# Linear attention feeding an MLP: the head of the program reordered, its transposes of batch 1 moved from DMA to TensorE, and later loads issued behind stages

## The chip, the cores and the metric

The kernel runs on one core of one Trainium2 chip. The time is device microseconds (us) of that core, as the median of the runs. Runs of one kernel mostly lie within 0.4% of their median. In these kernels the results of TensorE lie in PSUM, in tiles of one or two banks, until another engine takes them out (an eviction).

TensorE does matrix products and transposes, ScalarE (ACT in the profile) the exponentials, VectorE (DVE) maxima, divisions and copies, GpSimd (POOL) one multiply of the MLP and the scaling of v. GpSimd also issues the loads, and SyncE (SP) issues DMA transposes and output writes.

## The reference

```python
def phi(x):                                    # Hedgehog feature map
    proj = einsum('bhsd,df->bhsf', x, w_phi)   # 8 batches, 8 heads, seq 576, d 64, f 128
    proj = proj - max(abs(proj), axis=-1, keepdims=True)
    return concatenate([exp(proj), exp(-proj)], axis=-1)
q_p, k_p = phi(q), phi(k)
kv  = einsum('bhsf,bhsd->bhfd', k_p, v)
z   = sum(k_p, axis=2)
num = einsum('bhsf,bhfd->bhsd', q_p, kv)
den = einsum('bhsf,bhf->bhs', q_p, z)[..., None] + 1e-06
x   = (num / den).transpose(0, 2, 1, 3).reshape(4608, 512)
# then the MLP on all 4608 rows
h = x @ w_in                                   # 512 -> 2048
g = where(h > 0, h, exp(min(h, 0)) - 1)        # ELU
return g @ w_out                               # 2048 -> 512
```

## The kernel before

The heads are worked in 16 groups of four, two groups for each batch (n = 0 to 15, batch n // 2). The MLP is worked in nine chunks of 512 rows. For one group the stages are these: transpose k and q (so that d lies on the partitions); `stage_k` (project k, row maxima, exponentials, scale v); `stage_qmax` (project q only for its row maxima, split the maxima in two bf16 parts, transpose them to `mT`); `stage_q` (project q again, subtract the maxima by matmul, exponentials); `stage_kv`; `stage_pn` (numerator and denominator, divide, transpose x for the MLP).

```python
PE_TRANSPOSED = 2                    # groups 0 and 1 on TensorE, the others by DMA
pjp = psum_pool(bufs=2)              # two banks each: attention tiles
mpp = psum_pool(bufs=4)              # one bank each: MLP tiles

def pe_transpose(dst, blocks):       # on TensorE, in an attention tile
    tr = pjp.tile([P, 16, P], BF16, name="tr", tag="pj")
    for j, blk in enumerate(blocks):
        nc.tensor.transpose(tr[:, j, :], blk, ident)
    nc.vector.tensor_copy(dst, tr[:, 0:len(blocks), :])

# end of stage_qmax: the maxima of group n, transposed
if n < PE_TRANSPOSED:
    pe_transpose(mT, [mhl_2d])
else:
    nc.sync.dma_start_transpose(out=mT, in_=mhl_2d)

transposes(0)
for c in range(3): stage_k(0, c)
for c in range(3): stage_qmax(0, c)
transposes(1)
LAG = 3                              # an MLP chunk starts 3 pieces after its batch
for n in range(NG):
    pieces = []
    for c in range(3):
        pieces.append([(stage_q, n, c), (stage_qmax, n + 1, c)])
    pieces.append([(transposes, n + 2), (stage_kv, n)])
    pieces.append([(stage_k, n + 1, 0)])
    pieces.append([(stage_pn, n, 0)])
    pieces.append([(stage_k, n + 1, 1)])
    pieces.append([(stage_pn, n, 1)])
    pieces.append([(stage_k, n + 1, 2)])
    # loads of v of the next batch, k and q of the batch after it, are issued here
    # (on GpSimd; k, q and v have two buffers each)
    # after each piece, its share of 16 MLP pieces
    ...                              # cut: no n + 1 in the last group
```

An MLP piece is one first-layer tile (`moe_mm1`: four matmuls "ph", exponential on ScalarE, minimum on GpSimd, the rest of ELU on VectorE) or four second-layer matmuls (`moe_mm2`, "po"). A scheduler then orders each engine's instructions, and each engine takes them from its own queue.

## Time and profile before

| | us |
|---|---|
| median of 3 runs (lowest, highest) | 429.88 (429.65, 430.48) |
| span of the profiled execution | 429.5 |
| batch 0 complete: last copy of its transposed x ends | 68.9 |
| first q projection of group 2, 3, 4, 5 | 69.31, 89.76, 110.85, 132.94 |
| first q projection of group 15, the last | 346.57 |
| from there to the end (called the tail below) | 82.95 |

"First q projection" is the first matmul with the tile name pq of a group in the timeline. It is the milestone here. Here are the busy times from the page of the kernel before, and from its view of the DMAs (`--dma`) one group of issues; its last number is the median time from issue to landing.

```profile
PE 370.4 (86%) x3818; PEld 195.1 (45%) x3818; DVE 241.3 (56%) x405; ACT 246.5 (57%) x437; POOL 185.2 (43%) x249
...
mT<-mhl SPq DMA_TRANSPOSE x14, 3.7
```

The reader is to see that TensorE is the busiest engine with 370 of the 429.5 us of the span. The other 59 us are what a reordering can hope for, and they lie mostly in the first 75 us and in the waits between stages.

### The profile page before, as it was taken

To read this page: it belongs to the slowest core of one execution; us is meant where nothing else is said; L and a number is where in the kernel's file an instruction comes from. 1 tells how busy PE (TensorE), PEld (TensorE's weight loads), DVE (VectorE), ACT (ScalarE), POOL (GpSimd) and SP (SyncE) were. 2 spreads that over 40 slices of the span, in tenths; PEclk is the share of its full clock that TensorE was granted. 3 is DMA by queue.
4 is the path that set the end of the run, shared out by engine and by line. 5 is a ranking of instruction groups with operands and counts; after the bars stand their busy time and mean duration, and the time that the engine had idled before them with its cause. 6 is when DMAs were issued, how large, how long until landed. Compare 5 with 4: busy or idle time off the path is not lost.

```text
span 429.5 us, 9422 instructions
## 1 busy us (share of the span) xinstructions
PE 370.4 (86%) x3818; PEld 195.1 (45%) x3818; DVE 241.3 (56%) x405; ACT 246.5 (57%) x437; POOL 185.2 (43%) x249
## 2 busy tenths in 40 slices
PE   2467247889998999899989998999799989899995
PEld 2244233445453545354535453645354535344442
DVE  2646235876485648574857486648664853370630
ACT  1444416594777577747774777477657771451631
POOL 8612045382447245724572457145604570350620
PEclk9999657899999999999999999999999999999999
DMA  8999994359624982499259812853343003303113
GB/s 129 213 205 181 197 146 76 33 85 160 150 59 72 167 144 58 80 144 170 46 89 149 166 37 46 135 121 28 43 84 77 17 15 41 88 0 75 24 26 73
DMA packets 74619, 41.32 MB, mean 96 GB/s; under 512 B 54992, under 2 KB 69456, under 8 KB 74576
## 3 DMA queue, kind: packets, MB, share of 16 engines
q1 hardware_dynamic: 59232, 22.37, 29.1%
q0 software_dynamic: 15344, 18.35, 27.3%
q8 instruction: 30, 0.49, 0.5%
q14 instruction: 13, 0.11, 0.1%
HBM read 36.77 MB, written 9.44 MB: 108 GB/s over the span
## 4 chain that ended last, share of the span: by engine, by line
PE 51%; ACT 14%; POOL 11%; issue 11%; DVE 6%; DMA 6%; SPq 0%; POOLq 0%; ACTq 0%
PE po L185 21%; PE ph L163 14%; POOL e_sb L172 6%; ACT EK L270 5%; PE kv L372 5%; POOL vs L284 4%; DMA kT<-kn 4%; ACT e_sb L171 4%; ACT Eq L354 3%; PE pn L394 3%; PE pk L251 2%; PE pm L300 2%; DVE gT L175 2%; DVE mq L307 2%; DMA qn<-in_q_dram 1%
## 5 line engine op out<-in xcount | busy, mean ns | idle before, releaser
L163 PE MATMUL ph<-xT_sb,w_in_sb 128*128 128x512 bf16 x576 | 141.6, 385 | 14.3 <-DVE gT L175 12.9
L185 PE MATMUL po<-w_out_sb,gT 128*128 128x512 bf16 x576 | 137.8, 380 | 0.4 <-DVE gT L175 0.4
L175 DVE SCALAR_TENSOR_TENSOR gT<-e_sb,ph 128x512 bf16<-128x512 f32 x144 | 93.6, 683 | 65.6 <-POOL e_sb L172 65.6
L172 POOL TENSOR_SCALAR e_sb<-e_sb 128x512 f32<-128x512 f32 x144 | 86.5, 612 | 98.6 <-ACT e_sb L171 98.5
L171 ACT ACTIVATE e_sb<-ph 128x512 f32<-128x512 f32 x144 | 82.9, 608 | 45.8 <-PE ph L163 45.5
L284 POOL TENSOR_TENSOR vs<-vn,em 128x1152 bf16<-128x1152 bf16 x32 | 67.9, 2121 | 83.4 <-ACT em L281 83.3
L270 ACT ACTIVATE EK<-pk 128x768 bf16<-128x768 f32 x96 | 72.6, 813 | 35.7 <-DVE mk L242 35.6
L354 ACT ACTIVATE Eq<-pq 128x768 bf16<-128x768 f32 x96 | 74.0, 824 | 24.3 <-PE pq L344 24.2
L163 PEld LDWEIGHTS <-w_in_sb 128*128 128x128 bf16 x576 | 53.8, 99 | 72.6 <-issue 16.9
L185 PEld LDWEIGHTS <-gT 128*128 128x128 bf16 x576 | 52.2, 98 | 55.6 <-DVE gT L175 1.1
L307 DVE TENSOR_REDUCE mq<-pm 128x6 f32<-128x768 f32 x48 | 45.9, 957 | 49.5 <-PE pm L300 49.5
L194 ACT COPY o_sb<-po 128x512 f32<-128x512 f32 x36 | 21.1, 587 | 72.2 <-PE po L185 48.8
L242 DVE TENSOR_REDUCE mk<-pk 128x6 f32<-128x768 f32 x48 | 45.8, 953 | 12.4 <-PE pk L251 11.9
L394 PEld LDWEIGHTS <-Eq 128*128 128x128 bf16 x640 | 26.2, 102 | 8.4 <-issue 1.4
L251 PE MATMUL pk<-w_bd,kT 128*128 128x256 bf16 x144 | 26.3, 296 | 3.0 <-ACT EK L270 2.8
L372 PE MATMUL kv<-vs,EK 64*128 64x65 bf16 x1152 | 23.1, 198 | 5.3 <-POOL vs L290 4.2
L394 PE MATMUL pn<-kv_sb,Eq 128*128 128x65 bf16 x640 | 27.2, 200 | 0.3 <-DVE kv_sb L380 0.2
L300 PE MATMUL pm<-w_bd,qT 64*128 64x128 bf16 x288 | 18.0, 235 | 10.9 <-DMA qT<-qn 5.9
L406 DVE TENSOR_TENSOR xp<-pn,rec 128x640 bf16<-128x640 f32 x32 | 26.4, 824 | 1.1
L372 PEld LDWEIGHTS <-EK 64*128 64x128 bf16 x1152 | 20.9, 99 | 11.8 <-issue 4.3
L251 PEld LDWEIGHTS <-kT 128*128 128x128 bf16 x144 | 14.6, 105 | 15.5 <-issue 6.5
L334 PE MATMUL pq<-qT,w_bd 64*128 64x384 bf16 x96 | 17.2, 353 | 4.7 <-DVE mq L307 4.4
(42 smaller groups left out, 144.5 us busy)
## 6 DMA issues: line engine op xcount, KB each, us to landing
out_dram<-o_sb SPq DMA_DIRECT2D x72, 128.0 KB, 2.4
kn<-in_k_dram POOLq DMA_DIRECT2D x7, 576.0 KB, 6.1
qn<-in_q_dram POOLq DMA_DIRECT2D x7, 576.0 KB, 8.5
vn<-in_v_dram POOLq DMA_DIRECT2D x7, 576.0 KB, 6.7
w_in_sb<-in_moe_w_in_dram POOLq DMA_DIRECT2D x2, 1024.0 KB, 14.9
w_out_sb<-in_moe_w_out_dram POOLq DMA_DIRECT2D x2, 1024.0 KB, 31.4
xT_sb<-xp SPq DMA_TRANSPOSE x56, 2.4
kn<-in_k_dram POOLq DMA_DIRECT2D x2, 288.0 KB, 5.8
```

The source lines that it names most:

```text
L163: nc.tensor.matmul(ph, w_in_sb[:, ct, jt * P:(jt + 1) * P], xT_sb[:, ct, t0:t0 + CHUNK], start=(ct == 0), stop=(ct == N_CT - 1),)
L171: nc.scalar.activation(e_sb, ph, ACT.Exp)
L172: nc.gpsimd.tensor_scalar(e_sb, e_sb, 1.0, 0.0, op0=ALU.min, op1=ALU.max)
L175: nc.vector.scalar_tensor_tensor(gT[:, jt, :], e_sb, -1.0, ph, op0=ALU.add, op1=ALU.max)
L185: nc.tensor.matmul(po, gT[:, jt, tt * P:(tt + 1) * P], w_out_sb[:, jt, :], start=(jt == 0), stop=(jt == N_JT - 1),)
L251: nc.tensor.matmul(pj[:, 2 * i3:2 * i3 + 2, :].rearrange("p r f -> p (r f)"), kT[:, 3 * c + i3, :], w_bd.rearrange("p r f -> p (r f)"), st ...
L270: nc.scalar.activation(EK[:, sg, 6 * c:6 * c + 6, :], pj, ACT.Exp, scale=1.0 - 2.0 * sg)
L284: nc.gpsimd.tensor_tensor(vs[:, :, r, 0:D], natural["v", b][:, 2 * g + pr].unsqueeze(1).to_broadcast((P, 2, NS, D)), em[:, :, r].unsqueeze ...
L307: nc.vector.tensor_reduce(mq[:, 6 * c:6 * c + 6].rearrange("p (i r) -> p r i", r=2), pj[:, :, 0:3, :], axis=AX.X, op=ALU.max, apply_absolu ...
L354: nc.scalar.activation(Eq[:, sg, :, :, 3 * c * D:3 * (c + 1) * D].rearrange("p h r x -> p r h x"), pj[:, :, 0:3 * P].rearrange("p r (h x) ...
L372: nc.tensor.matmul(kv[:, hi, pr, sg, :], EK[rows, sg, pr * NS + s, :], vs[rows, sg, pr * NS + s, :], start=(s == 0), stop=(s == NS - 1),)
L394: nc.tensor.matmul(pn[:, hi, t, :], Eq[:, sg, hi, par, i0 * D:(i0 + 2) * D], kv_sb[:, hi, pr, sg, :], start=(sg == 0), stop=(sg == 1),)
```

## The change

The intent is to fill the loose first 75 us. The head becomes serial: batch 0 is run to its end first, so that the MLP can start early. Batch 1 (groups 2 and 3) is transposed on TensorE too, now in the MLP's PSUM banks, in parts of five. The k and q maxima of group 2 become a stage of their own with 4 MLP pieces. The loads of later batches are issued behind the stages that free their buffers. In the loop the piece with the transposes and kv is cut in two. In the last group, which has nothing to transpose, this leaves an empty piece, which only moves MLP pieces: those between kv and pn.

```diff
-    PE_TRANSPOSED = 2
+    PE_TRANSPOSED = 4
+    PE_TRANSPOSED_X = 2          # x of groups 0 and 1 on TensorE, as before
 ...
     def pe_transpose(dst, blocks):
-        tr = pjp.tile([P, 16, P], BF16, name="tr", tag="pj")
-        for j, blk in enumerate(blocks):
-            nc.tensor.transpose(tr[:, j, :], blk, ident)
-        nc.vector.tensor_copy(dst, tr[:, 0:len(blocks), :])
+        for j0 in range(0, len(blocks), 5):
+            part = blocks[j0:j0 + 5]
+            tr = mpp.tile([P, 8, P], BF16, name="tr", tag="mp")
+            for j, blk in enumerate(part):
+                nc.tensor.transpose(tr[:, j, :], blk, ident)
+            nc.vector.tensor_copy(dst[:, j0:j0 + len(part), :], tr[:, 0:len(part), :])
 ...
+    run(
+        [[(transpose_in, 0, "k")]] + thirds(stage_k, 0)
+        + [[(transpose_in, 0, "q")]] + thirds(stage_qmax, 0)
+        + [[(transpose_in, 1, "k")]] + thirds(stage_k, 1)
+        + thirds(stage_q, 0) + [[(transpose_in, 1, "q")]] + thirds(stage_qmax, 1)
+        + [[(stage_kv, 0)], [(stage_pn, 0, 0)], [(stage_pn, 0, 1)]]
+        + thirds(stage_q, 1)
+        + [[(stage_kv, 1)], [(stage_pn, 1, 0)], [(stage_pn, 1, 1)]],
+        0,                       # no MLP pieces yet
+    )
+    batch_done(0, 1)             # the chunk of batch 0 starts 1 piece later
+    run(
+        [[(transpose_in, 2, "k")]] + thirds(stage_k, 2)
+        + [[(transpose_in, 2, "q")]] + thirds(stage_qmax, 2)
+        + [[(transpose_in, 3, "k")], [(transpose_in, 3, "q")]],
+        4,                       # with 4 MLP pieces
+    )
+    load("k", k, 2)
+    load("q", q, 2)
+    load("v", v, 2)
-    for n in range(NG):
+    for n in range(2, NG):
 ...
-        pieces.append([(transposes, n + 2), (stage_kv, n)])
+        pieces.append([(stage_kv, n)])
+        pieces.append([(transpose_in, n + 2, "k"), (transpose_in, n + 2, "q")])
         if nxt:
-            pieces.append([(stage_k, n + 1, 0)])
+            pieces[-1].append((stage_k, n + 1, 0))
         pieces.append([(stage_pn, n, 0)])
+        if g == 0 and b + 2 < B:
+            pieces[-1].append((load, "k", k, b + 2))
+            pieces[-1].append((load, "q", q, b + 2))
+        if g == 1 and b + 2 < B:
+            pieces[-1].append((load, "v", v, b + 2))
 ...
-        if g == 0 and b > 0 and b + 1 < B:
-            load("v", v, b + 1)
-        if g == 0 and b + 2 < B:
-            load("k", k, b + 2)
-            load("q", q, b + 2)
 ...
+        run(pieces, 16 if n > 2 else 12)
```

"..." marks cuts (helpers, the loop of MLP pieces, which `run` now holds unchanged, and the x transposes of groups 0 and 1, which also use MLP banks now).

More of the change, by code (lines that the diff above doesn't have):

```diff
@@ L221, in pe_transpose, with transpose_in @@
     def pe_transpose(dst, blocks):
-        tr = pjp.tile([P, 16, P], BF16, name="tr", tag="pj")
-        for j, blk in enumerate(blocks):
-            nc.tensor.transpose(tr[:, j, :], blk, ident)
-        nc.vector.tensor_copy(dst, tr[:, 0:len(blocks), :])
-    def transposes(n, names=("k", "q")):
+        for j0 in range(0, len(blocks), 5):
[4 more added lines that the diff above has]
+            nc.vector.tensor_copy(dst[:, j0:j0 + len(part), :], tr[:, 0:len(part), :])
+    def transpose_in(n, name):
         if n >= NG:
@@ L231, in transposes @@
         b, g = divmod(n, 2)
-        for name in names:
-            nat = natural[name, b][:, 2 * g:2 * g + 2].rearrange("p r s d -> p (r s d)")
-            dst = tpool.tile([P, NI, P], BF16, name=name + "T")
-            if n < PE_TRANSPOSED:
-                pe_transpose(dst, [nat[:, i * P:(i + 1) * P] for i in range(NI)])
-            else:
-                nc.sync.dma_start_transpose(out=dst, in_=nat)
-            st[name + "T", n] = dst
+        nat = natural[name, b][:, 2 * g:2 * g + 2].rearrange("p r s d -> p (r s d)")
+        dst = tpool.tile([P, NI, P], BF16, name=name + "T")
+        if n < PE_TRANSPOSED:
+            pe_transpose(dst, [nat[:, i * P:(i + 1) * P] for i in range(NI)])
+        else:
+            nc.sync.dma_start_transpose(out=dst, in_=nat)
+        st[name + "T", n] = dst
     def row_max(m, pj, c):
@@ L416, in stage_pn @@
         mixed = xT_sb[:, ct, mixed_col(b):mixed_col(b) + D]
-        if n < PE_TRANSPOSED:
-            tr = pjp.tile([P, 16, P], BF16, name="trx", tag="pj")
+        if n < PE_TRANSPOSED_X:
+            tr = mpp.tile([P, 8, P], BF16, name="trx", tag="mp")
             for t in range(5):
@@ L431, in stage_pn @@
             )
-    transposes(0)
-    for c in range(3):
-        stage_k(0, c)
-    for c in range(3):
-        stage_qmax(0, c)
-    transposes(1)
     LAG = 3
@@ L448, in after_piece, with run, batch_done, thirds @@
                 timers.remove(t)
-    for n in range(NG):
+    def run(pieces, atoms):
+        done = 0
+        for j, piece in enumerate(pieces):
+            for fn, *args in piece:
+                fn(*args)
+            after_piece()
+            while done < atoms * (j + 1) // len(pieces):
+                emit_moe()
+                done += 1
+    def batch_done(b, lag):
+        for ch in range(N_CHUNK):
+            tiles = range(ch * 4, ch * 4 + 4)
+            if max(2 * (t // 9) + (1 if t % 9 >= 4 else 0) for t in tiles) == b:
+                timers.append([lag, ch])
+    def thirds(stage, n):
+        return [[(stage, n, c)] for c in range(3)]
+    run(
[19 more added lines that the diff above has]
+    for n in range(2, NG):
         b, g = divmod(n, 2)
@@ L467 @@
             pieces.append([(stage_k, n + 1, 2)])
-        if g == 0 and b > 0 and b + 1 < B:
-            load("v", v, b + 1)
-        if g == 0 and b + 2 < B:
-            load("k", k, b + 2)
-            load("q", q, b + 2)
-        done = 0
-        for j, piece in enumerate(pieces):
-            for fn, *args in piece:
-                fn(*args)
-            after_piece()
-            want = 16 * (j + 1) // len(pieces)
-            while done < want:
-                emit_moe()
-                done += 1
+        run(pieces, 16 if n > 2 else 12)
         if g == 1:
-            for ch in range(N_CHUNK):
-                tiles = range(ch * 4, ch * 4 + 4)
-                if max(2 * (t // 9) + (1 if t % 9 >= 4 else 0) for t in tiles) == b:
-                    timers.append([LAG if nxt else 0, ch])
+            batch_done(b, LAG if nxt else 0)
     after_piece()
```

## The prediction

> **What bounds the kernel now.** I read the page's slices first: TensorE is 90% busy or more from the eighth slice on, and 20 to 80% before.
>
> ```profile
> PE   2467247889998999899989998999799989899995
> PEclk9999657899999999999999999999999999999999
> DMA  8999994359624982499259812853343003303113
> ```
>
> One slice is 10.7 us, so the first 75 us (the head) are the loose part, and the DMA engines are full there. The timeline shows the rest is even: the q projection of head group n starts at 69.31 us for n=2, 89.76 for n=3, 110.85 for n=4, 132.94 for n=5 and 346.57 for n=15: 21.3 us a step from n=5 on. From 369.79 us TensorE alone ends it (two MLP chunks, 253 matmuls at 0.216 us).
>
> So the change can only pay in the head. The chain of waits, over 0 to 120 us, has one long piece there:
>
> ```profile
> 40.05 0.32 DVE xT_sb L423
> 40.37 14.56 DMA kT<-kn
> 54.93 0.03 issue
> 54.96 0.04 POOLq L71
> 55.00 0.49 issue
> 55.50 0.80 POOL kn L71
> 56.30 0.02 issue
> 56.32 2.13 POOL vs L284
> 58.45 0.20 POOL vs L290
> 58.66 0.04 issue
> 58.70 1.17 PE kv L372 x36
> ```
>
> Read it downwards: the DMA transpose of k for group 3, issued at 40.37, lands at 54.93. GpSimd stands at the load of batch 3's k, which overwrites the transpose's source; behind that load, in program order, is the v scaling of group 1, and kv of group 1 needs it. The waits up to 100 us have the same line (`POOL kn L71 <- DMA kT<-kn`, 13.7 us), and TensorE also waits 5.9 us for a transpose of q. Batch 0's last transposed x, which lets the MLP start, is copied at 68.68 us. From 42 to 58 us TensorE does 4 us of work.
>
> The granted clock, in stretches of 2 us, shows a second cost:
>
> ```profile
> 46.00:48.00 2.00, 0.00 (x0) 0.00 (x0) 0.00 (x0) 0.00 (x0) 0.00 (x0) 0.50 1.21 197
> 68.00:70.00 2.00, 2.00 (x17) 0.95 (x16) 1.48 (x3) 0.58 (x2) 1.79 (x2) 0.69 0.00 0
> ```
>
> The column after the five engines is the clock: half from about 45.4 to 69.3 us. Durations say that it was also half before 38.5 us, although the slices show 9 there: 72 kv matmuls take 2.16 us at 29.7 us and 1.33 us at 80.3 us.
>
> **What the Trainium skill says.** "TensorE: Matmul & The Clock Gate", Part 1, says that the array has two clocks, half and full, and that a window of about 3.4 us, idle or busy, switches them. The trace agrees: half clock begins 3 us after the idle time began at 42.1 us, and full clock returns at 69.3 after a dense stretch. Its Part 4 says that transposes do not engage the full clock; here five x transposes take 0.71 us at the half clock and 0.45 us at 39.56 us, so they profit from it; whether they count as activity no run shows. "DMA: Bandwidth & Descriptors", Issuing engines are not separate DMA queues, says that all DMAs share 16 engines. The trace agrees: issue to landing of the head's transposes is 12.6, 17.7 and 14.6 us beside the weight loads, 3.3 us (median of all for k) later. The first page, Part 1, also calls GpSimd a strict FIFO; the 13.7 us above are that.
>
> **The change part by part.**
>
> Removed: the DMA transposes of k and q for groups 2 and 3 and of two of the row maxima of q (mT). Batch 1 goes through TensorE, so the loads that overwrite k and q of batch 1 wait for TensorE alone; and in the instruction order they stand behind the v scaling of group 2. The 14.6 us wait and the 5.9 us wait have no counterpart left.
>
> Added: 36 transposes for k and q and 2 for the maxima at 0.065 us (full clock) to 0.125 us (half), 2.5 to 4.7 us of TensorE, and their copies, 0.76 us per 1152 columns now, about 0.85 in two halves: 3.4 us of VectorE. They lie between 50 and 66 us, mostly on the path.
>
> Moved: before, k and q maxima of group n+1 run inside group n. Now batch 0 is run first (both k, then both q), and k and q maxima of group 2 follow as a stage of their own with 4 MLP pieces. The wait is gone, but so is an overlap.
>
> Walk of the new order with the old durations. A projection tile (TensorE to first ScalarE or VectorE use) costs 0.86 us at the half clock and 0.55 at full; a maximum 0.96; a pair of exponentials 1.51; kv 2.1 or 1.26; 40 pn matmuls 2.4 or 1.25; the division of one pn 1.25. The projections keep two PSUM buffers, so each waits for the exponentials or the maximum two tiles ahead.
> - First k projection at 8.8 us: two q transposes stand ahead of it and q lands at 8.5. Before 9.49.
> - k of group 0 ends (ScalarE) at 15.9, q maxima at 18.1 (before 19.6; the 1.35 us copy of the selector now follows them).
> - Transposes of group 1 18.6 to 20.9, its k exponentials 22.8 to 28.0, q of group 0 to 32.5, q maxima of group 1 35.4.
> - kv of group 0 36.6, pn and division 41.4; x stands at 42 (before 40.6). Then q of group 1 46.1, kv 46 to 46.7, pn, division, x transposes: batch 0 complete at 51 (full clock from about 42) to 53 (half). Before 68.7: a gain of 16 to 17 us.
> - Now the lost overlap. k transposes and copies of group 2, one MLP tile (its exponential stands ahead of k's on ScalarE), three pairs of k exponentials to 58.8, the maxima to 61.7 (two of them wait for those exponentials' buffers), and transposes of group 3, which share four PSUM banks with the MLP tiles and so wait for an MLP eviction at about 65. The first q exponential of group 2 starts at 67 (full clock) or 69.5 (half), before 69.92. **Of the 16 us, 13 to 15 are given back.**
> - Group 2: the same stage plus 12 MLP tiles (before 13), 20 us in both, VectorE the closest (12 evictions of 0.683, maxima 5.8, division and copies 4). Group 3 starts at 87 to 89.5, before 89.76: gain 2.8 or 0.3.
> - By then 16 MLP pieces are done instead of 13, so group 3 is 16 second-layer pieces, with ScalarE light: about 20.6 us against 21.1. Group 4 holds 13 pieces instead of 16: 20.3 us, as group 2 took (20.45 with 13), against 22.1. Gain 2.3.
> - From the middle of group 4 the order on all engines is the old one except for some second-layer matmuls in the last step: no more gain.
>
> Sum: 2.8 + 2.3 = 5.1 us with full clock from about 42 us, 0.3 + 2.3 = 2.6 with half until about 57 us. If the dense stretch at 18.6 to 22.3 us (transposes and k of group 1) brings the full clock already there, kv and pn of group 0 and some projections lose some 2 us more: 7. I take 4.4: 429.9 - 4.4 = 425.5.
>
> **The rivals.**
> 1. *The 16 us come through.* For it: batch 0 is complete that much earlier, and the chain gave that wait 14.6 us. Against: the steps advance with the attention, not with the MLP, and at 68.7 us the old kernel had k and q maxima of group 2 already behind it. The time would be 415 to 418. I hold it unlikely.
> 2. *The new stage is worse than I walk it.* MLP tiles and transposes share four banks, GpSimd's loads of k and q of batch 3 wait for TensorE's transposes of group 3 with MLP minima behind them. Then the first q exponential of group 2 comes after 70 us and the time is 429 to 432. For it: my 67 has three engines waiting in turn. Against: group 4's shorter step remains.
> 3. *Loads.* k, q and v of batch 2 are now issued behind four v scalings, at about 30 us, and land behind w_out. Now w_out lands at 40.0 and 47.6 us, and k and q of batch 2 at 51.2 and 54.7, with transposes beside them; without these they should end no later than 55, and the DMA transposes of group 4 need them after 55. Hidden in either case: 0 us.
>
> **Range and chances.** The clock decides between -2.6 and -7; the walk has some 60 waits and may be 3 us off either way. Range 420.5 to 429.5. Faster by over 2% means under 421.3: 0.14, the early clock and a better stage together, or rival 1. Slower by over 2% (over 438.5) needs a new long wait: 0.02. Within 2%: 0.84.
>
> **What would show each step right or wrong.** In the chain of the changed kernel no transpose by DMA before 65 us and no GpSimd load with a long wait. Batch 0's last x copy at 51 to 53 us; first q exponential of group 2 at 66 to 70; group 3's q at 86 to 90; group 5's q projection 2.6 to 7 us ahead of 132.94, and that lead equal to the gain in time. The granted clock full from 42 or 57 us, without a later drop. The prediction is wrong if the lead at group 5 is much over 7 us (I overrated the lost overlap), if the clock stays half past 60 us, or if lead and gain differ (then the steady part or the tail changed).

## More of the kernel before

The 14 transposes of mT (and 14 each of k and q) are groups 2 to 15.

## The result, and the profile after

The changed kernel takes 426.85 us (median of 4 runs, 425.78 to 427.19), against 430.18 us of the kernel before in the same rounds. The ratio is 0.9917, with a 95% interval of 0.9894 to 0.9941. Ratios here are the mean time of one kernel's fast runs over that of the other's of the same rounds, so not quite the ratio of the medians. This lies inside the predicted range, 1.35 us above the predicted 425.5. The medians differ by 3.3 us. The two traces below differ by 4.4, because the profiled execution of the kernel before is a slow one (431.30 us, 1.1 above the median), while that of the changed kernel (426.88) lies at its median.

The slices of the changed kernel's page (the span in 40, one is 10.6 us) answer to those in the prediction.

```profile
PE   3447747999998999899989998999799989999995
...
PEclk9965878799999999999999999999999999999999
```

The fifth and sixth slices (43 to 64 us) now read 7 and 4 for TensorE where they read 2 and 4. But the sixth is still low, and the clock still has a 7 in the sixth and the eighth slice. The head is fuller, yet not full.

This is the chain of waits of the changed kernel at 49 to 66 us: start, duration, what.

```profile
49.98 0.45 PE trx L422 x5
50.44 0.50 PE tr L228 x9
...
59.79 1.75 DVE mq L309 x2
...
64.01 1.49 PE tr L228 x14
```

The 14.56 us line of a DMA transpose is gone, and no long GpSimd line stands in its place. Batch 0 is complete at 51.0 us (the last x transposes at 49.98, then their copies), before 68.9. From 50.4 on the chain runs through the new stage: transposes, exponentials and maxima of group 2, then transposes of group 3, and so to q of group 2. Its first exponential starts at 67.94, before at 69.92. **So 17.9 us were gained and 15.9 given back**, much as predicted (16 to 17 and 13 to 15).

The milestones side by side, from the timelines:

| first q projection of | before | after | gain |
|---|---|---|---|
| group 3 | 89.76 | 89.59 | 0.2 |
| group 4 | 110.85 | 110.02 | 0.8 |
| group 5 | 132.94 | 130.79 | 2.2 |
| group 15 | 346.57 | 344.49 | 2.1 |
| end of the span | 429.52 | 425.07 | 4.4 |

How far can single executions be trusted? Two runs below, e2 and e7, go through the same sequence of instructions as the kernel before up to the last group (compared on ScalarE, VectorE, GpSimd and SyncE, since some records of TensorE are missing), and their q of group 3 comes at 88.65 and 88.29, of group 5 at 131.84 and 131.47. So a milestone scatters by some 1.5 us from one execution to the next. From group 3 to group 5 all three take 43.2 us, and the changed kernel takes 41.2; lengths of this kind are steadier than starts.

The gain comes from three places: 0.2 us, less than the scatter, from the whole head with group 2, 2.0 us from groups 3 and 4, and, in the tail, 2.4 us that nothing in the prediction explains. Group 2 itself is odd: q of group 3 comes 21.7 us after the first q exponential of group 2, where 20 were predicted. The timeline of TensorE in the changed kernel shows what stands in it. A line is start, duration, engine, instruction, and in brackets the idle time before it with its releaser.

```profile
70.10 0.39 PE L164 MATMUL ph<-xT_sb,w_in_sb 128*128 128x512 bf16 x1
71.61 0.34 PE L336 MATMUL pq<-qT,w_bd 64*128 64x384 bf16 x2 [1.11 <-ACT Eq L356]
...
73.72 0.73 PE L374 MATMUL kv<-vs,EK 64*128 64x65 bf16 x19 [1.10 <-ACT Eq L356]
74.82 0.29 PE L228 MATMUL tr<-ident,mhl 128*128 128x128 bf16 x1 [0.37 <-DVE mhl L318]
...
75.33 3.19 PE L164 MATMUL ph<-xT_sb,w_in_sb 128*128 128x512 bf16 x7 [0.22 <-issue]
```

The transpose of the maxima of group 3 waits for mhl, the last step of the q maxima of group 3. In TensorE's instruction order eight MLP matmuls, two tiles, stand directly behind it (the trace has records of seven), so from 70.5 to 75.3 us no MLP matmul starts. TensorE itself is idle for only 0.37 us in front of the transpose. But it idles for 1.11 and 1.10 us more in front of pq and kv, which wait for exponentials, and the MLP matmuls that could fill these waits stand behind the transpose. A bank is not what holds them, though the transpose takes one of the MLP's four: if the banks go round in turn, those two tiles get the banks of tiles whose evictions on VectorE start at 69.08 and 70.66 us and take 0.7 us each. ScalarE, in the same timeline, has no MLP tile for 5.4 us:

```profile
71.44 0.60 ACT L172 ACTIVATE e_sb<-ph 128x512 f32<-128x512 f32 x1
...
76.85 0.60 ACT L172 ACTIVATE e_sb<-ph 128x512 f32<-128x512 f32 x1 [3.19 <-PE ph L164]
```

Group 2 must carry 12 MLP tiles through ScalarE, GpSimd and VectorE, and a gap in that row is a candidate for the 1.7 us too many. The granted clock is the other candidate. Here it is in windows of 3.4 us, in the same form as in the prediction (the clock follows the five engines):

```profile
52.70:56.10 3.40, 1.73 (x17) 0.89 (x16) 3.35 (x6) 3.40 (x8) 0.61 (x1) 1.00 0.00 0
56.10:59.50 3.40, 0.95 (x18) 0.53 (x18) 1.41 (x3) 2.14 (x6) 3.26 (x4) 0.99 0.46 87
...
69.80:73.20 3.40, 1.54 (x29) 0.86 (x23) 1.98 (x3) 3.19 (x6) 1.22 (x2) 0.98 1.19 203
73.20:76.60 3.40, 2.29 (x23) 1.26 (x25) 1.72 (x5) 0.46 (x1) 0.00 (x0) 0.50 0.60 103
```

The clock falls to half at 59.5 and again at 73.2, each time after a window in which TensorE was busy less than half the time (0.95 and 1.54 of 3.4 us). The seven MLP matmuls at 75.33 take 3.19 us because of it.

The tail, at last. SyncE's queue and the last wait of TensorE before its long run, in the timeline of the kernel before and then of the changed one:

```profile
362.19 2.53 SPq L429 DMA_TRANSPOSE xT_sb<-xp  x1
...
364.81 1.18 SPq L196 DMA_DIRECT2D out_dram<-o_sb  x2
...
366.08 1.25 SPq L426 DMA_TRANSPOSE xT_sb<-xp  x1
...
369.79 4.49 PE L163 MATMUL ph<-xT_sb,w_in_sb 128*128 128x512 bf16 x20 [1.16 <-DMA xT_sb<-xp]
```

```profile
361.61 1.22 SPq L428 DMA_TRANSPOSE xT_sb<-xp  x1
...
362.87 1.22 SPq L431 DMA_TRANSPOSE xT_sb<-xp  x1
...
364.18 2.81 SPq L197 DMA_DIRECT2D out_dram<-o_sb  x4
...
365.03 9.23 PE L164 MATMUL ph<-xT_sb,w_in_sb 128*128 128x512 bf16 x41
```

Before, one issue took 2.53 us instead of 1.2, two output writes stood ahead of the last pair of x transposes, and TensorE waited 1.16 us for them. After, the transposes go out in a row (the first two at 359.01 and 360.30) ahead of the writes, and the wait is gone. The empty piece in the last group moved the writes.

### The profile page after: what moved, and what is told of

Read it like the earlier page. It is cut to its first block, busy times and chain, and to the rows that moved or that the text cites. A ratio compares the mean times of both kernels' runs of the same rounds, so it can differ in the third digit from the quotient of the medians.

```text
span 425.1 us, 9444 instructions
## 1 busy us (share of the span) xinstructions
PE 367.0 (86%) x3803; PEld 198.2 (47%) x3856; DVE 245.1 (58%) x419; ACT 245.8 (58%) x437; POOL 185.1 (44%) x249
## 4 chain that ended last, share of the span: by engine, by line
PE 51%; ACT 14%; POOL 12%; issue 12%; DVE 9%; DMA 1%; POOLq 0%; ACTq 0%
PE po L186 21%; PE ph L164 16%; POOL e_sb L173 6%; ACT EK L272 6%; POOL vs L286 5%; PE kv L374 4%; ACT Eq L356 4%; DVE mq L309 3%; DVE gT L176 3%; ACT e_sb L172 3%; PE pn L396 2%; PE pm L302 2%; PE pk L253 2%; PE tr L228 1%; DMA qn<-in_q_dram 1%
## 5 line engine op out<-in xcount | busy, mean ns | idle before, releaser
L164 PE MATMUL ph<-xT_sb,w_in_sb 128*128 128x512 bf16 x551 | 137.9, 384 | 11.7 <-DVE gT L176 9.2
L186 PE MATMUL po<-w_out_sb,gT 128*128 128x512 bf16 x548 | 131.5, 379 | 3.4 <-issue 2.7
L176 DVE SCALAR_TENSOR_TENSOR gT<-e_sb,ph 128x512 bf16<-128x512 f32 x144 | 94.0, 683 | 68.9 <-POOL e_sb L173 68.7
L356 ACT ACTIVATE Eq<-pq 128x768 bf16<-128x768 f32 x96 | 73.3, 826 | 15.9 <-PE pq L346 15.6
L309 DVE TENSOR_REDUCE mq<-pm 128x6 f32<-128x768 f32 x48 | 45.6, 956 | 41.2 <-PE pm L302 41.2
L253 PE MATMUL pk<-w_bd,kT 128*128 128x256 bf16 x144 | 24.7, 287 | 5.0 <-ACT EK L272 4.9
L396 PEld LDWEIGHTS <-Eq 128*128 128x128 bf16 x640 | 24.8, 100 | 8.8 <-issue 1.3
L396 PE MATMUL pn<-kv_sb,Eq 128*128 128x65 bf16 x640 | 25.8, 197 | 1.8 <-DVE kv_sb L382 1.8
L374 PEld LDWEIGHTS <-EK 64*128 64x128 bf16 x1152 | 21.8, 101 | 9.8 <-ACT Eq L356 4.4
L374 PE MATMUL kv<-vs,EK 64*128 64x65 bf16 x1152 | 24.2, 200 | 2.5 <-ACT Eq L356 1.7
L302 PE MATMUL pm<-w_bd,qT 64*128 64x128 bf16 x288 | 17.0, 227 | 8.2 <-ACT EK L272 3.6
L253 PEld LDWEIGHTS <-kT 128*128 128x128 bf16 x144 | 14.6, 103 | 17.9 <-issue 8.5
```

The lines of the kernel that those rows point to most:

```text
L164: nc.tensor.matmul(ph, w_in_sb[:, ct, jt * P:(jt + 1) * P], xT_sb[:, ct, t0:t0 + CHUNK], start=(ct == 0), stop=(ct == N_CT - 1),)
L176: nc.vector.scalar_tensor_tensor(gT[:, jt, :], e_sb, -1.0, ph, op0=ALU.add, op1=ALU.max)
L186: nc.tensor.matmul(po, gT[:, jt, tt * P:(tt + 1) * P], w_out_sb[:, jt, :], start=(jt == 0), stop=(jt == N_JT - 1),)
L253: nc.tensor.matmul(pj[:, 2 * i3:2 * i3 + 2, :].rearrange("p r f -> p (r f)"), kT[:, 3 * c + i3, :], w_bd.rearrange("p r f -> p (r f)"), st ...
L309: nc.vector.tensor_reduce(mq[:, 6 * c:6 * c + 6].rearrange("p (i r) -> p r i", r=2), pj[:, :, 0:3, :], axis=AX.X, op=ALU.max, apply_absolu ...
L356: nc.scalar.activation(Eq[:, sg, :, :, 3 * c * D:3 * (c + 1) * D].rearrange("p h r x -> p r h x"), pj[:, :, 0:3 * P].rearrange("p r (h x) ...
```

## The experiments

The theory that I started from has two parts. The new order of the head is what gives the gain back, so TensorE's transposes in the old order should keep most of it. And the tail gains through the empty piece. The rivals: a different wait holds group 3 wherever group 2 starts; the clock does it; the loads alone do it.

This table has every run. "Before" ran in the same rounds (medians 429.95 for e1 to e4, 430.33 for e5 to e8, 430.76 for e9 to e11). The milestones are of the one profiled execution, with the scatter named above.

| run | median us (lowest, highest) | ratio to before, 95% | q of group 2 | group 3 | group 5 | tail |
|---|---|---|---|---|---|---|
| before | 429.88 (429.65, 430.48) | | 69.31 | 89.76 | 132.94 | 82.95 |
| after | 426.85 (425.78, 427.19) | 0.9917 (0.9894, 0.9941) | 60.71 | 89.59 | 130.79 | 80.58 |
| e1_old_order | 426.77 (425.61, 427.92) | 0.9927 (0.9904, 0.9949) | 61.43 | 88.68 | 131.13 | 81.30 |
| e2_loads_only | 429.88 (429.32, 430.94) | 1.0003 (0.9982, 1.0024) | 68.67 | 88.65 | 131.84 | 82.49 |
| e3_old_tail | 428.41 (424.65, 430.48) | 0.9956 (0.9914, 0.9999) | 64.00 | 90.31 | 131.75 | 81.29 |
| e4_warm | 432.51 (429.02, 433.67) | 1.0042 (1.0007, 1.0078) | 60.17 | 88.45 | 133.53 | 80.60 |
| e5_old_order_lag1 | 427.84 (426.64, 429.55) | 0.9945 (0.9924, 0.9966) | 59.82 | 89.29 | 131.13 | 81.27 |
| e6_lag1_new_tail | 427.07 (426.07, 428.66) | 0.9929 (0.9909, 0.9949) | 60.15 | 89.52 | 130.24 | 80.57 |
| e7_before_new_tail | 428.85 (427.82, 429.50) | 0.9967 (0.9948, 0.9985) | 68.23 | 88.29 | 131.47 | 81.42 |
| e8_own_buffer | 450.47 (449.28, 451.66) | 1.0470 (1.0435, 1.0505) | 62.70 | 86.56 | 133.10 | |
| e9_after_mt3 | 422.17 (420.16, 424.46) | 0.9809 (0.9776, 0.9842) | 60.03 | 83.56 | 124.68 | 80.53 |
| e10_combined | 420.12 (418.84, 423.50) | 0.9769 (0.9737, 0.9801) | 58.87 | 82.50 | 123.25 | 80.48 |
| e11_kq_dma | 437.49 (435.97, 438.98) | 1.0167 (1.0136, 1.0198) | 69.76 | 96.41 | 139.46 | 81.43 |

In the kernels with the new order (after, e3, e4, e9, e11) the first pq matmuls of group 2 can run well ahead of the rest: the first exponential follows only at 67.94 in the changed kernel and at 67.30 in e9, but at 62.35 in e1.

### e1_old_order: the old order of the head, with the rest of the change

The kernel before, with the transposes of batch 1 on TensorE in MLP banks and the late loads:

```diff
-    PE_TRANSPOSED = 2
+    PE_TRANSPOSED = 4
+    PE_TRANSPOSED_X = 2
 ...                              # pe_transpose as in the change
+        if g == 0 and b + 2 < B: # loads behind stage_pn(n, 0), as in the change
 ...
```

> The change without its reordering: TensorE transposes for batch 1 in the MLP banks and later loads, but k and q maxima of group n+1 still inside group n. Theory (the serial stage for group 2 gives back most of what the removed waits bring): group 1 starts at about 40 us as before, takes a waitless 18 to 19 us at the half clock, group 2's q projection starts at 58 to 60 us against 69.3 (before) and about 67 (changed), group 5 starts about 10 us before 132.94, time 419 to 422 us, some 5 to 8 us below the changed kernel. Rival (the reordering costs nothing, what limits the head are the shared banks and the half clock): within 1.5 us of the changed kernel, 425.5 to 428.

Group 2's first exponential came at 62.35, 5.6 us earlier than in the changed kernel, near to what the theory said. But q of group 3 came at 88.68, and the time is that of the changed kernel, which is the rival's number. The theory's time is refuted: **5.6 us of lead at group 2 left 0.9 at group 3**, which is within the scatter. In e1 the MLP starts late (first tile at 70.4, its chunk waits three pieces), with the same transpose ahead of it:

```profile
70.35 0.29 PE L228 MATMUL tr<-ident,mhl 128*128 128x128 bf16 x1
...
70.43 3.34 PE L164 MATMUL ph<-xT_sb,w_in_sb 128*128 128x512 bf16 x8
```

### e2_loads_only: the kernel before with only the late loads

```diff
         pieces.append([(stage_pn, n, 0)])
+        if g == 0 and b + 2 < B:
+            pieces[-1].append((load, "k", k, b + 2))
+            pieces[-1].append((load, "q", q, b + 2))
+        if g == 1 and b + 2 < B:
+            pieces[-1].append((load, "v", v, b + 2))
 ...
-        if g == 0 and b > 0 and b + 1 < B:
-            load("v", v, b + 1)
-        if g == 0 and b + 2 < B:
-            load("k", k, b + 2)
-            load("q", q, b + 2)
```

> The old kernel with only its later loads moved behind the first division of each group; transposes of batch 1 stay DMAs. Theory: GpSimd's 13.7 us wait goes, but kv of group 1 then waits for the q maxima of group 2 and their DMA transpose (landing at 48), so only about 4 us come out: group 2 starts at 65, time 425.5 to 427. Rival 1 of the prediction (that wait is the whole loss): 415 to 418.

The time did not move (ratio 1.0003), and the chain of waits shows why:

```profile
38.44 16.30 DMA kT<-kn
...
55.30 0.80 POOL kn L71
56.13 2.13 POOL vs L284
```

The scheduler put the load of batch 3's k back in the same place of GpSimd's queue, ahead of group 1's v scaling. In the two traces GpSimd, SyncE, ScalarE and VectorE go through the same sequence of instructions as before. So this run does not tell what moved loads are worth once they really move; it tells that this edit alone is inert.

### e3_old_tail: the changed kernel without the empty piece

```diff
         pieces.append([(stage_kv, n)])
-        pieces.append([(transpose_in, n + 2, "k"), (transpose_in, n + 2, "q")])
+        if nxt:
+            pieces.append([(transpose_in, n + 2, "k"), (transpose_in, n + 2, "q")])
```

> The changed kernel, but the last group has no empty piece between kv and the divisions, so its pieces are cut as before. Theory (2.4 of the gain arose in the last step, where the new cut takes an output write from ahead of the last x transposes on the SP queue): 2 to 2.5 us slower than the changed kernel, about 429, with an output write again ahead of the last two transposes and TensorE idle before the last two chunks. Rival (the 2.4 us between the traces are lost records and run-to-run spread): within 0.7 us of the changed kernel.

The total scatters (424.65 to 430.48), so its interval overlaps that of the changed kernel and settles nothing. The tail, which is read inside one execution, grew from 80.58 to 81.29: 0.7 us, a third of what I expected. So the cut of the last group is one part of the 2.4 us, not all of it.

### e4_warm: the changed kernel with filler matmuls that keep the clock up

Eight matmuls on each half of each q-maximum tile of groups 2 and 3 and of each q tile of group 2, into columns that nothing reads (144 in all):

```diff
+        for par in range(2):
+            for _ in range(8):
+                nc.tensor.matmul(pj[:, par, 3 * P:4 * P], ident, w_bd[:, par, :],
+                                 start=True, stop=True)
```

> The changed kernel plus 144 unneeded matmuls (128 rows, 128 columns) into unused columns of the projection tiles of groups 2 and 3, to keep the clock. Theory (the two stretches of half clock at 59.5 to 66.3 and 73.2 to 80.0 us are on the path and cost 2 to 3 us): clock full from 46 us on, group 3's q 2 to 3 us before 89.6, time 424 to 425. Rival (the head waits on ScalarE, VectorE and GpSimd, the clock matters little): within 0.7 us of the changed kernel or slower by up to 1, with the clock full all the same.

The record shows the full clock from 43.0 to 114.7 us, and still q of group 3 came only 1.1 us earlier (88.45 against 89.59). So the clock, net of what the fillers cost, was worth some 1 us there, no more than the scatter, and it is not what holds group 3. The total is worse. In the trace this comes from a later wait that the fillers did not aim at: the transpose of x that the next chunk needs landed late.

```profile
108.78 5.02 DMA xT_sb<-xp
```

It is issued while a load of q, issued at 105.44, is under way; 5.0 us compares with a median of 2.4 us. That the load delays it is argued, not shown. The trace is of one of the two faster executions (429.60 us); what the other four, at 432.5 to 433.7, lost beyond it is in no trace.

### e5_old_order_lag1: e1 with the first MLP chunk queued earlier

```diff
-                    timers.append([LAG if nxt else 0, ch])
+                    timers.append([1 if b == 0 else LAG if nxt else 0, ch])
```

> The old-order kernel of the earlier run with one more edit: batch 0's MLP chunk is queued one piece after batch 0 ends instead of three. There group 2 began at 61.4 us (before 69.3) but group 3 only at 88.7: its first MLP matmul ran at 70.6, after 9 us of group 2. Theory (what bounds the next 20 us is the row of MLP evictions, so an early batch 0 pays only if the MLP starts with it): first MLP matmul at about 62 to 63 us, group 3's q at 82 to 84, group 5's at 124 to 127, time 419 to 422. Rival (group 2 is slow because TensorE is at the half clock to 73 us): group 3 at 87 to 89 again, time within 1.5 us of 426.8.

The MLP now starts at 61.0 us, 9 us earlier than in e1, and q of group 3 comes at 89.29. The late MLP start was not the cause either, and the theory is refuted (427.84 us, not 419 to 422). But the timeline has a gap in the MLP's exponentials as the changed kernel has, from one at 66.21 to the next at 72.23:

```profile
70.20 0.29 PE L228 MATMUL tr<-ident,mhl 128*128 128x128 bf16 x1 [1.11 <-DVE mhl L319]
...
72.23 0.60 ACT L172 ACTIVATE e_sb<-ph 128x512 f32<-128x512 f32 x1 [3.81 <-PE ph L164]
```

In seven kernels so far (before, after, e1 to e5) q of group 2 had started anywhere from 60 to 69 us, and group 3 always came at 88.4 to 90.4. The five of them that start it early (after, e1, e3, e4, e5) all transpose group 3's maxima on TensorE, in front of MLP work. This gave the theory of e9.

### e6_lag1_new_tail and e7_before_new_tail: the empty piece alone, on e5 and on the kernel before

Both add the same two lines:

```diff
         pieces.append([(transposes, n + 2), (stage_kv, n)])
+        if not nxt:
+            pieces.append([])
```

> The kernel before this one in the call plus an empty piece in the last group, which gives the changed kernel's cut of the last step. Theory of the tail: 2 us (1.5 to 2.5) below it, from last q projection to end 80.6 instead of 82.5 to 83; no output write ahead of the last two x transposes. Rival: no difference above 0.7 us. If the early MLP start works as well, this is the fastest of all, 417 to 420.

> The old kernel plus that empty piece in the last group, nothing else. Theory: 428 (1.5 to 2.5 below the old kernel), all of it after the last group's first q projection at 346.6. Rival (the difference between the two traces was chance): 429.5 to 430.5.

e6 against e5: the tail went from 81.27 to 80.57, again 0.7 us and not the 2 expected, and the time is far from 417 to 420. e7 against before: the median fell by 1.5 us (428.85 against 430.33; ratio 0.9967, interval 0.9948 to 0.9985), and the tail from 82.95 to 81.42. The cut of the last group alone is thus a real gain on the kernel before, and it has nothing to do with the head.

A second part stays. In e7 one issue of an x transpose on SyncE is long again, and TensorE still waits for the transfer:

```profile
359.65 2.10 SPq L426 DMA_TRANSPOSE xT_sb<-xp  x1
...
366.79 7.51 PE L163 MATMUL ph<-xT_sb,w_in_sb 128*128 128x512 bf16 x33 [0.31 <-DMA xT_sb<-xp]
```

In all five kernels that transpose k and q of batch 1 by DMA (before, e2, e7, e8 and e11, the last with the new order) such a long issue (2.06 to 2.53 us) falls on the x transposes of the last group. In the other eight, whose queue of SyncE has fewer DMAs ahead of that place, none there is longer than 1.25 us. e11, which is the changed kernel with four DMA transposes more in the head, has a tail of 81.43 instead of 80.58. What makes one issue long is not settled; only that where it falls differs with what stood in the queue before.

### e8_own_buffer: the kernel before, with k of batch 1 in a buffer of its own

This takes away what GpSimd's load waits for, without moving any transpose. To make room, the output tiles had to be cut from three buffers to one and the x tiles from three to two:

```diff
-            natural[name, b] = io.tile([P, H // 2, NS, D], BF16, name=name + "n")
+            natural[name, b] = io.tile([P, H // 2, NS, D], BF16,
+                **(dict(name="k1", bufs=1) if (name, b) == ("k", 1)
+                   else dict(name=name + "n")))
```

> The old kernel with a buffer of its own for k of batch 1, so that the load of k of batch 3 needn't wait for the DMA transposes (to make room, one output buffer instead of three and two x buffers instead of three, so its total is not to be compared; the head is read from the trace; the TensorE order is the old one). Theory: GpSimd no longer waits, v scaling of group 1 ends by 46 us, but kv of group 1 then waits for the q maxima of group 2 at about 53.4, whose q transposes land at 48: group 2's q at 65 to 66.5 (old 69.3), so 3 to 4 of the 14.6 us. Rival 1 of the prediction (the wait is the loss): group 2's q at 54 to 57.

Its total (450.47) is not to be compared, for it has fewer output and x buffers, and later steps are longer (from group 6 to 7 26.9 us, before 22.1). In the head, group 2 starts at 62.70, 6.6 us earlier than before, so the load's wait was real: more than the 3 to 4 us that I expected, and far from the 54 to 57 of rival 1. But the next one took its place, the load of q behind the DMA transpose of q:

```profile
51.18 12.47 DMA qT<-qn
...
64.23 0.72 POOL qn L75
```

With the maxima's transpose on DMA, group 3 came at 86.56, outside the band of 88.4 to 90.4 (e7 just leaves it with 88.29): a first sign for the theory, though in a kernel that differs in more than this.

### e9_after_mt3: the changed kernel with one transpose, that of group 3's maxima, by DMA

```diff
-        if n < PE_TRANSPOSED:
+        if n < PE_TRANSPOSED - 1:
             pe_transpose(mT, [mhl_2d])
```

> The changed kernel, but the row maxima of q of group 3 (one 128x128 tile) are transposed by a DMA again instead of on TensorE. Theory: in the traces of all kernels with that transpose on TensorE, TensorE stands in front of it inside group 2 (waiting for the maxima) with the MLP's matmuls queued behind, and no MLP eviction runs for some 4 to 5 us (changed kernel: none from 72.8 to 76.9 us); the DMA has the whole rest of the group to land. So group 3's q comes 1.5 to 4 us before 89.6, group 5's as much before 130.8, time 423.5 to 425.5. Rival (group 2 waits for other things, the half clock or the row of evictions): within 1 us of 426.85.

One transpose moved to another queue, and q of group 3 comes at 83.56, 6.0 us earlier; group 5 is 6.1 us earlier and so is the end of the profiled span (419.0 against 425.1). The median is 422.17, better than expected (423.5 to 425.5), with more scatter (420.16 to 424.46). The ratios to before are 0.9809 and 0.9917, 1.1% apart, some 4.6 us; the intervals (0.9776 to 0.9842, 0.9894 to 0.9941) do not meet. TensorE and ScalarE in its timeline:

```profile
69.47 1.47 PE L164 MATMUL ph<-xT_sb,w_in_sb 128*128 128x512 bf16 x6
...
72.14 1.24 PE L164 MATMUL ph<-xT_sb,w_in_sb 128*128 128x512 bf16 x5 [0.16 <-issue]
...
73.14 0.65 ACT L172 ACTIVATE e_sb<-ph 128x512 f32<-128x512 f32 x1
75.05 0.60 ACT L172 ACTIVATE e_sb<-ph 128x512 f32<-128x512 f32 x1 [1.25 <-PE kv L374]
```

Six MLP matmuls run at 69.47 and five at 72.14, where the changed kernel has one, at 70.10, and then none until 75.33; the widest gap of the exponentials between 73 and 79 us is 1.9 us instead of 5.4. The transpose itself takes longer by DMA (its issue alone 1.87 us at 74.77, against 0.29 us on TensorE), but its result is needed only for q of group 3, 9 us later. The clock, too, stays full from 66 us on in e9, so the 6.0 us contain what the half clock from 73.2 to 80.0 cost the changed kernel. The theory is confirmed, and the gain is larger than the 1.5 to 4 us that I expected. What is shown is that this one transpose on TensorE costs the 6 us; that it does so by its place in the queue is read from the two traces.

### e10_combined: the old order of the head with everything learned

e6 (old order, k and q of batch 1 on TensorE, late loads, early MLP, empty piece), with the maxima by DMA from group 2 on:

```diff
-        if n < PE_TRANSPOSED:
+        if n < 2:
             pe_transpose(mT, [mhl_2d])
```

> Old order, k and q of batch 1 on TensorE, all row maxima after batch 0 by DMA, late loads, MLP one piece after batch 0, new cut of the last step. Theory (the old-order kernels had group 2 at 60 but group 3 at 89 because TensorE stood 5 us before that transpose and the MLP behind it): group 2 at 58 to 60, group 3 at 83 to 86, group 5 at 124 to 127, time 419 to 422.5, the fastest of all. Rival (16 first-layer pieces beside a group take 27 to 29 us whatever the start): group 3 at 87 to 90, group 5 at 129 to 131, time 425 to 427.

It takes 420.12 us, with a ratio of 0.9769 (0.9737 to 0.9801), **2.3% under the kernel before and the fastest of all**; the interval ends just past the 2% mark (0.98), so by the rule it is "unclear" whether it is 2% faster. Compared with e6 this edit moved group 3 from 89.52 to 82.50, the same effect as in e9, in the other order of the head. With that wait gone the old order does as well as the new one or slightly better: 420.12 against 422.17 in the same rounds with overlapping intervals, and 1.1 us at group 3 and 1.4 at group 5 in the profiled executions, within their scatter. So the serial head is not what the gain needs.

### e11_kq_dma: the changed kernel with k and q of batch 1 transposed by DMA again

```diff
-        if n < PE_TRANSPOSED:
+        if n < PE_TRANSPOSED_X:
             pe_transpose(dst, [nat[:, i * P:(i + 1) * P] for i in range(NI)])
```

> The changed kernel, but k and q of batch 1 are transposed by DMA (as before the change); the row maxima stay on TensorE. Theory: in the new order batch 1 is first needed at 50 us and its loads land at 27 and 30, so the DMA transposes of group 2 are hidden; those of group 3 wait for buffers and are also done by 60 us; 38 transposes and 3.4 us of VectorE copies leave the stage between 50 and 66 us, so group 2's q starts 1 to 3 us before 60.7 to 67.9 (first exponential 65 to 67), time 424.5 to 426.5. Rival (the loads of k and q of batch 3 wait for these DMAs on GpSimd ahead of v scalings, as in the old kernel): 427 to 431.

The time is 437.49, 1.7% over the kernel before and some 10.6 us over the changed kernel's median. Theory and rival both expected less, 424.5 to 426.5 and 427 to 431; the rival had the cause. The wait is back in the chain:

```profile
45.23 18.52 DMA qT<-qn
```

GpSimd stands at the load of q of batch 3 until 63.8 us, and group 3 comes at 96.41. So the transposes on TensorE are the essential part of the change, and without them the serial head is worse than the old one.

## Why the prediction was right or wrong

The time and the range were right: 426.85 us against a predicted 425.5. But this was luck. The 4.4 us that I took were some 2.1 won before group 3 starts and 2.3 in groups 3 and 4, and nothing after. The traces show 0.2, 2.0 and 2.4 in the tail: one term came to almost nothing, and a gain that the prediction had ruled out took its place. Two of the signs that it named for being wrong came true: the clock fell to half at 59.5 us and was half until 66.3, and the lead at group 5 (2.2 us) is not the gain at the end (4.4). One reading was loose too: from the eighth slice on the digits of TensorE are mostly 8 and 9, not 9 throughout.

- **The removed wait: right.** Batch 0 was complete at 51.0 us (predicted 51 to 53), and no GpSimd load waited long. The first DMA transpose was issued at 55.1 us; none stands in the chain before 65 us, as I wrote. e11 shows the wait's return when the transposes go back to DMA.
- **The lost overlap: right.** First q exponential of group 2 at 67.94 (predicted 67 to 69.5). Rival 1, all 16 us coming through, is refuted. e1 shows more: avoiding the lost overlap would not have helped by itself, because group 3 was held by something else.
- **Group 2, "the same stage plus 12 MLP tiles, 20 us in both": wrong.** It took 21.7 us, and q of group 3 came at 89.59, just outside 87 to 89.5. The step counted the two added transposes of the maxima as 0.13 to 0.25 us of TensorE work and put no wait on them. What one of them did was to stand in TensorE's queue behind the last q maximum, with eight MLP matmuls behind it that could have filled TensorE's waits. e9 measures it: 6.0 us at group 3. Without it group 2 takes 16.3 us from its first exponential, so the 20 us that I took over from the kernel before were no fixed length of the stage either. Rival 2 looked for such a thing in the new stage; it came one stage later, and it is in the old order too (e1, e5).
- **The clock: wrong.** I expected the full clock from 42 or 57 us without a drop. It came at 45.9, fell at 59.5, returned at 66.3 and fell again from 73.2 to 80.0. e4 shows some 1 us at group 3 for it, net of the fillers and within the scatter.
- **Groups 3 and 4: right.** The gain between q of group 3 and q of group 5 is 2.0 us, predicted 2.3 (0.5 for group 3 and 1.8 for group 4); the steps were 20.43 and 20.77 us, predicted 20.6 and 20.3.
- **"No more gain" from group 4 on: wrong.** The lead of 2.2 us at group 5, already under the least predicted (2.6), stayed 2.1 until group 15; then the tail gave 2.4 us. The step dismissed the last group ("except for some second-layer matmuls in the last step"). Of the 2.4 us, 0.7 are the cut of the last group (e3, e6; on the kernel before itself it is worth 1.5, e7). Most of the rest goes with a long DMA issue, 2.53 us instead of 1.2, that no longer falls on the last x transposes once batch 1 is off the DMA queue (e11 brings it back); why that issue is long is open.
- **Loads, rival 3: right.** None of the chain's waits in the head is for a load of batch 2. How much late loads help by themselves was not shown, since e2 did not move them.

What stays open: the cause of the long issues on SyncE, and what moved loads alone would give.

## What to carry to other kernels

In this kernel a small instruction was priced by what stands behind it in its queue, not by its duration: a transpose whose operand comes late and whose result is needed a stage later belongs on a queue in which nothing urgent waits (here DMA: 6.0 us at group 3, some 4.6 us of the time), while transposes that free a buffer for the next load belong on the engine that does them at once (here TensorE, some 10 us better). When a change frees 18 us and the time falls by 3, look at the next milestone that does not move, whatever the earlier one does, and ask which instruction all those kernels share. And check the end of the program after any re-cut of a loop: here an empty piece in the last step was worth 1.5 us by itself (e7).

## What the Trainium skill lacked or had wrong

- "VectorE: DVE Perf Modes", The three transpose paths, gives 390 ns for a 128x128 transpose on TensorE and 1309 ns by DMA, and its rules for kernel authors advise TensorE if the result may go to PSUM. The single transposes are ordered likewise here (0.29 us in the record of TensorE; a median of 3.7 us from issue to landing by DMA), yet the program with the DMA is 6.0 us ahead at group 3 (e9). The page lacks the cost of what stands behind the transpose in its queue.
- "TensorE: Matmul & The Clock Gate", Part 1, speaks of an idle window that brings the half clock. In the changed kernel it came after windows in which TensorE was busy for 1.54 and 0.95 of 3.4 us, and did not come after one with 1.73 us (the windows are placed by the switches seen). Which share decides is on no page.
- "DMA: Bandwidth & Descriptors" does not say why, among transposes issued by SyncE, a single issue takes twice as long as the others of its kind. Here most x transposes take 1.2 us to issue, and single ones at the tail 2.06 to 2.53 us.
